# Batch 3's local q and k: transposed by DMA and reordered from SBUF, instead of transposed on TensorE

## The chip, the core and the metric

The kernel runs on one core of a Trainium2 chip. The metric is the device time of one execution in microseconds, the median of several runs. All engines of the core work from their own queues of instructions and wait for each other by semaphores: TensorE (PE, with its weight loads PEld), VectorE (DVE), ScalarE (ACT), GpSimd (POOL), which also issues the loads that cast from fp32 to bf16, and SyncE (SP), which issues DMA transposes and output stores.

## What is computed

Sparse attention over 8 batches, 8 heads, 576 tokens, 64 channels, then a feed-forward layer without bias over all 4608 tokens:

```python
scores = scale * np.matmul(q, k.transpose(0, 1, 3, 2))
rel = pos[:, None] - pos[None, :]
mask_local = (rel >= 0) & (rel < 32)                                   # heads 0 to 3
mask_strided = (rel >= 0) & (pos[None, :] % 32 == pos[:, None] % 32)   # heads 4 to 7
attn = softmax(np.where(masks, scores, -1e9))
x = np.matmul(attn, v)                  # tokens x 512
h = np.maximum(x @ w_in, 0.0)           # 512 -> 2048
out = (h * h) @ w_out                   # 2048 -> 512
```

Inputs and output are fp32; the kernel computes in bf16 with fp32 sums.

## The kernel before

A unit is a pair of heads of one batch, number 4 b + p for batch b and pair p. Pairs 0 and 1 are local (unit 12 and 13 in batch 3), pairs 2 and 3 strided. Attention writes its result, channels on partitions, into four tiles `xt`, one per pair, with 576 columns per batch. The feed-forward layer reads `xt` in nine chunks of 512 tokens.

The main loop is a list of 288 groups of four matmuls of 128x512: for each chunk 16 groups `mm1` (L707: `xt` by `w_in`; ACT's relu L713 and DVE's square L714 follow) and 16 groups `mm2` (L729: by `w_out`; after each four groups ACT copies the sum to a tile `y` at L733 and SP stores it at L737). `mm1` uses two PSUM banks in turn. Groups 32 to 47 are `mm1` of chunk 1, 48 to 63 `mm2` of chunk 1, and group 64 begins `mm1` of chunk 2.

The attention is written by hand between these groups. `PLAN` has lines "group: words", and each word runs a step just before the group's matmuls; every engine then takes its instructions in that order. A unit or batch stands behind the letter, then q or k, then the engine (a ACT, v DVE). The words that matter here:

- `l3k12+13`, `l3q12+13` (L290): POOL loads q or k of units 12 and 13 with a cast to bf16 into unused columns of `xt`, six tokens on a partition.
- `c12qa` (`cast_qk_local`, L297): ACT or DVE copies one unit's rows into a tile `q_l` or `k_l`, heads side by side.
- `T12qa` (`step_T`, L453, L460): six TensorE transposes of 96x128 into a PSUM bank, then a copy that puts the tokens in order into `qT` or `kTl`, channels on partitions.
- `S12!` (L505, L521, L527): scores of a local unit, exponentials on ACT, masks on DVE; `D12.0`, `D12.1` (L667, L672, L673) multiply by v and divide; `E12` (L682) brings the result into `xt`, for batches from 2 on by a DMA transpose on SP.
- `C3q`, `C3k` (L349): POOL loads of the strided heads' rows of a batch into one tile each for q and k, used by all batches in turn; `X3q`, `X3k` (L354): their DMA transposes on SP into `qT_s` and `kT_s`; `k30v`, `k31v` (L365, L368): DVE's copies into `kb`; `s3.0` to `s3.2` (L574): the strided scores; `x3.0` to `x3.2` (L585 to L604): the sums, their inverse and the product with v into `xt`.
- `Q16k` and the like (L278), `Y16` (L378): from batch 4 on, local q and k are loaded one token on a partition and transposed by DMA straight into place.
- `V` and `U`: loads of v; `B`: spreading them.

Tile pools hold four `q_l`, four `k_l` and four `qT`; `kTl` is four tiles, chosen by `v_slot`, `(b * 2 + p % 2) % NV`.

Of the kernel before, what the change touches and what calls it, by code (L numbers as in the profile page):

```python
# [9 lines left out]
BF16 = mybir.dt.bfloat16  # L10
# [18 lines left out]
6: o2 l2k8+9 mv0g o3 mk0g  # L29
10: c4qv  # L30
11: c4kv
12: l2q8+9 T4qa
13: c5qv c5ka T4kv
14: W1q0v T5qa
15: S4!
16: W1q1v T5ka
# [14 lines left out]
35: T8kv  # L51
37: T9kv
38: T8qv C3k
41: S8!
42: T9qa
44: S9! D8.0 k20v
45: D8.1 k21v
46: B20v
47: E8 D9.0 B21v U3
48: Q16k s2.0  # L60
49: D9.1
50: Q17q Q16q c12kv s2.1
51: c12qa E9 s2.2
52: Q17k c13kv c13qa
54: x2.0
55: X3q X3k
56: x2.1 C4k C4q
57: T12ka
58: V4 T13qv T12qa
59: T13ka  # L70
60: x2.2 B30v
61: B31v
63: U4 S12!
# [83 lines left out]
def kernel(  # L157
# [9 lines left out]
    nc = tc.nc  # L167
    B, H, S, D = q.shape
    d_model, d_ff = moe_w_in.shape
    T = B * S  # L170
# [3 lines left out]
    QL = 96  # L174
# [15 lines left out]
    qkT = ctx.enter_context(tc.tile_pool(name="qkT", bufs=4))  # L190
# [17 lines left out]
    def bank(nm):  # L208
        if places:
            return all_banks[places.pop(0)]  # L210
        t = banks[nm].pop(0)
        banks[nm].append(t)
        while id(t) in unread:
            run_due(lambda x: x[1] == unread[id(t)])
        return t
# [10 lines left out]
    NV = 4  # L226
# [12 lines left out]
    kTl = [singles.tile([128, 32 + S], BF16, name=f"kTl{i}") for i in range(NV)]  # L239
# [18 lines left out]
    units = [(b, p) for b in range(B) for p in range(H // 2)]  # L258
    st = {}
# [34 lines left out]
    def cast_qk_local(u, name, copy):  # L294
        s = st[u]
        t = qk_in.tile([QL, 6, 2, D], BF16, name=f"{name}_l")
        copy(t.rearrange("p j h d -> p h j d"), s[name + "f"].rearrange("p h (j d) -> p h j d", j=6))  # L297
        s[name] = t
# [16 lines left out]
    def step_TS(b, name, g, copy):  # L315
        src = str_rows[b, name]
        pt = bank("pt").bitcast(BF16)[:, 0:S]
        if b:
            for i in range(NJ):
                c = 128 * (NJ * g + i)  # L320
                nc.tensor.transpose(pt[:, SP_ * i:SP_ * (i + 1)], src[:, c:c + 128], ident[0:SP_, 0:SP_])
            if g == 0:
                o = strTs[name].tile([128, NP2 * SR], BF16, name=f"{name}T_s")
                str_T[b, name] = o.rearrange("c (a p) -> c a p", p=SR)
            copy(str_T[b, name][:, NJ * g:NJ * (g + 1), 0:SP_], pt.rearrange("c (a p) -> c a p", p=SP_))
            return
        for i in range(2):
            for s3 in range(NP3):
                c = 128 * (2 * g + i)
                o = S // 2 * i + QL * s3  # L330
                nc.tensor.transpose(pt[:, o:o + QL], src[:, s3, c:c + 128], ident[0:QL, 0:QL])
        if g == 0:
            o = strTs[name].tile([128, 2 * NJ * SR], BF16, name=f"{name}T_s")
            str_T[b, name] = o[:, 0:2 * NJ * SP_].rearrange("c (a r) -> c a r", a=NJ // 2)
        o = str_T[b, name]
        copy(o[:, 2 * g:2 * g + 2, :].rearrange("c a r -> c (a r)"), pt)
        if g == 1:
            for i in range(2):
                st.setdefault(2 + i, {})[name + "T"] = \
                    o[:, :, 2 * SP_ * i:2 * SP_ * (i + 1)].rearrange("c a (h p) -> c h a p", h=2)  # L340
# [11 lines left out]
    def transpose_str(b, name):  # L352
        o = strTs[name].tile([128, NP2 * SR], BF16, name=f"{name}T_s").rearrange("c (a p) -> c a p", p=SR)
        nc.sync.dma_start_transpose(out=o, in_=big.pop((b, name)))  # L354
        str_T[b, name] = o
# [14 lines left out]
    def transpose_local(u):  # L370
        s = st[u]
        for name in "qk":
            if name == "k":
                full = kTl[v_slot(u)]
                dst = full[:, 32:32 + S]
            else:
                full = dst = qkT.tile([128, S], BF16, name="qT")
            nc.sync.dma_start_transpose(out=dst.rearrange("c (t p) -> c t p", p=QL),  # L378
                                        in_=s[name].rearrange("p t h d -> p (t h d)"))
            s[name + "T"] = full  # L380

    def v_slot(u):
        b, p = units[u]
        return (b * 2 + p % 2) % NV
# [63 lines left out]
    def step_T(u, name, copy):  # L448
        s = st[u]
        src = s[name].rearrange("p j h d -> p (j h d)")  # L450
        pt = bank("pt").bitcast(BF16)[:, 0:S]
        for j in range(6):
            nc.tensor.transpose(pt[:, QL * j:QL * (j + 1)], src[:, 128 * j:128 * (j + 1)],  # L453
                                ident[0:QL, 0:QL])
        if name == "k":
            full = kTl[v_slot(u)]
            dst = full[:, 32:32 + S]
        else:
            full = dst = qkT.tile([128, S], BF16, name="qT")
        copy(dst.rearrange("c (p j) -> c p j", j=6), pt.rearrange("c (j p) -> c p j", j=6))  # L460
        s[name + "T"] = full
# [6 lines left out]
    def step_B(u, half):  # L468

        local = is_local(u)  # L470
        kn = 128 if local else SP_
        pair, both = biased[u, half] = bank_pair()
        bias = bias_l[:, half].rearrange("p t c -> p (t c)") if local else bias_s.rearrange("p t c -> p (t c)")
        for ps in pair:
            nc.tensor.matmul(ps[0:kn, 0:S // 2], ident[0:kn, 0:kn], bias,  # L475
                             start=True, stop=False, skip_group_check=True)
# [263 lines left out]
    A, V, G = nc.scalar.copy, nc.vector.tensor_copy, nc.gpsimd.tensor_copy  # L740
    ENG = {"a": A, "v": V, "g": G}
# [18 lines left out]
    def warm(n):  # L760
        if n:
            pw = bank("py")
            for _ in range(n):
                nc.tensor.matmul(pw, idle[:, 0:128], idle, start=True, stop=True)
# [7 lines left out]
    def run_step(word):  # L772
        word, _, at = word.partition("/")
        places[:] = [int(x) for x in at.split(",") if x]
        op, arg = word[0], word[1:]
        if op == "w":
            warm(int(arg))
        elif op == "c":
            cast_qk_local(int(arg[:-2]), arg[-2], ENG[arg[-1]])
        elif op == "T":  # L780
            step_T(int(arg[:-2]), arg[-2], ENG[arg[-1]])
        elif op == "W":
            step_TS(int(arg[0]), arg[1], int(arg[2]), ENG[arg[3]])
        elif op == "S":
            u, _, half = arg.rstrip("!").partition(".")
            step_S(int(u), int("!" in arg), [int(half)] if half else range(2))
        elif op == "G":
            step_G(int(arg))
        elif op == "b":
            step_B(*(int(x) for x in arg.split(".")))  # L790
        elif op == "N":
            step_N(int(arg))
        elif op == "O":
            step_O(int(arg))
        elif op in "sx":
            (step_SS if op == "s" else step_XX)(*(int(x) for x in arg.split(".")))
        elif op == "k":
            step_K(int(arg[0]), int(arg[1]), ENG[arg[2]])
        elif op == "m":
            memset_later(arg[:-1], nc.gpsimd if arg[-1] == "g" else nc.vector)  # L800
        elif op == "D":
            if "." in arg:
                u, part = arg.split(".")
                step_D(int(u), int(part))
            else:
                step_D0(int(arg))
        elif op == "E":
            step_E(int(arg.rstrip("av")), ENG.get(arg[-1]))
        elif op == "P":
            first_part(*([int(x) for x in y] for y in arg.split(".")))  # L810
        elif op == "H":
            shift_v_local(int(arg[:-1]), ENG[arg[-1]])
        elif op == "C":
            load_str_tall(int(arg[:-1]), arg[-1])
        elif op == "Q":
            load_qk_rows(int(arg[:-1]), arg[-1])
        elif op == "X":
            transpose_str(int(arg[:-1]), arg[-1])
        elif op == "Y":
            transpose_local(int(arg))  # L820
        elif op == "V":
            load_v_local_all(int(arg))
        elif op == "U":
            load_v_str(int(arg))
        elif op == "B":
            spread_v_str(int(arg[0]), int(arg[1]), ENG[arg[2]])
        elif op == "l":
            load_qk_local_sw(int(arg[0]), [int(x) for x in arg[2:].split("+")], arg[1])
        elif op == "r":
            load_str_rows(int(arg[0]), arg[1])  # L830
        elif op == "i":
            load_w_in(int(arg))
        elif op == "o":
            load_w_out(int(arg))
        elif op == "z":
            late_constants()
        else:
            raise ValueError(word)
# [143 lines left out]
```

## Time and profile before

| | |
|---|---|
| median of 3 runs | 299.3 us (299.23 to 299.55) |
| profiled execution, own time | 300.02 us |
| its span | 298.3 us |
| granted TensorE clock | 1.00 |
| PE busy | 289.5 us |
| DVE, ACT, POOL busy | 176.6, 172.2, 74.1 us |
| q0, q1: packets | 54448, 38512 |

The page gives busy times per engine over the span, the span in 40 slices of 7.46 us, the DMA queues (q0 carries POOL's loads, q1 SP's transposes and stores), the chain of waits that ended last, and the costliest groups of instructions by line. A timeline line has start, length, engine, line, operation and, in brackets, the idle time before it and what ended it. Instructions that follow each other are merged, with their number behind an x.

### The profile page before, as it was taken

The page shows a single profiled execution, that of the slowest core. Times are in us where ns is not written, and L with a number is a line of the kernel's source. Part 1 is how long each engine was busy: PE and PEld are TensorE (multiplying, and loading weights), DVE is VectorE, ACT ScalarE, POOL GpSimd, SP SyncE. Part 2 cuts the span into 40 slices and gives each one's busy share as a digit, 9 for nine tenths or more (in the row PEclk, how much of TensorE's full clock was granted, in tenths as well). Part 3 has the DMA queues.
Part 4 walks back from the last instruction along what each step waited for, and adds up shares of the span by engine and source line. Part 5 has one row for each costly group of instructions (what it writes and reads, how often), then busy time and mean ns, then how long its engine had stood idle before and what let it go on. Part 6 is the DMA issues. An engine that isn't in the chain of part 4 may idle for free.

```text
span 298.3 us, 5654 instructions
## 1 busy us (share of the span) xinstructions
PE 289.5 (97%) x2136; PEld 146.0 (49%) x2172; DVE 176.6 (59%) x457; ACT 172.2 (58%) x324; POOL 74.1 (25%) x107
## 2 busy tenths in 40 slices
PE   7989999999999999999999999999999999999996
PEld 2644555544544544444455445544454444444445
DVE  6657689668768694598267945685484534104400
ACT  3758846696667735773477547645665257126511
POOL 8973743005404008138303800000000000000000
PEclk9999999999999999999999999999999999999999
DMA  7999999999999999999997998621011110010012
GB/s 146 188 208 205 193 199 185 145 196 160 133 155 191 152 155 175 146 155 175 199 194 120 171 190 120 108 57 70 35 23 54 66 43 0 35 74 35 0 70 73
DMA packets 93131, 37.28 MB, mean 125 GB/s; under 512 B 78956, under 2 KB 87238, under 8 KB 93104
## 3 DMA queue, kind: packets, MB, share of 16 engines
q0 software_dynamic: 54448, 18.82, 59.1%
q1 hardware_dynamic: 38512, 18.03, 31.7%
q8 instruction: 17, 0.28, 0.4%
q14 instruction: 10, 0.08, 0.1%
q10 hardware_dynamic: 144, 0.07, 0.1%
HBM read 38.21 MB, written 9.44 MB: 160 GB/s over the span
## 4 chain that ended last, share of the span: by engine, by line
PE 89%; DMA 6%; issue 2%; ACT 1%; DVE 1%; SPq 0%; POOL 0%; DVEq 0%; ACTq 0%; POOLq 0%
PE psb L729 40%; PE psb L707 37%; DMA qT_s<-q_t 4%; DMA w_out_b<-in_k_dram 2%; PE psb L667 2%; PE psb L574 1%; PE psb L588 1%; PE psb L754 1%; PE psb L585 1%; PE psb L453 1%; PE psb L505 1%; PE psb L550 1%; ACT r L713 1%; DVE xt L635 0%; PE psb L475 0%
## 5 line engine op out<-in xcount | busy, mean ns | idle before, releaser
L707 PE MATMUL psb<-xt,w_in_b 128*128 128x512 bf16 x558 | 132.1, 379 | 1.2 <-DVE xt L635 0.2
L729 PE MATMUL psb<-w_out_b,g_sb 128*128 128x512 bf16 x542 | 125.3, 379 | 1.3 <-issue 0.6
L713 ACT ACTIVATE r<-psb 128x512 bf16<-128x512 f32 x144 | 85.5, 600 | 37.5 <-PE psb L707 34.0
L714 DVE TENSOR_TENSOR g_sb<-r 128x512 bf16<-128x512 bf16 x144 | 60.8, 424 | 73.6 <-ACT r L713 72.8
L707 PEld LDWEIGHTS <-w_in_b 128*128 128x128 bf16 x576 | 53.4, 98 | 58.8 <-issue 1.3
L729 PEld LDWEIGHTS <-g_sb 128*128 128x128 bf16 x560 | 51.8, 98 | 57.3 <-DVE g_sb L714 0.3
L733 ACT COPY y<-psb 128x512 f32<-128x512 f32 x35 | 20.6, 590 | 53.2 <-PE psb L729 50.2
L598 DVE TENSOR_TENSOR xt<-psb,rv 64x144 bf16<-64x144 f32 x84 | 34.1, 406 | 9.0 <-ACT rv L591 7.9
L590 ACT ACTIVATE rv<-psb 128x432 f32<-128x432 f32 (+1 forms) x21 | 10.5, 500 | 9.8 <-PE psb L585 9.8
L673 DVE TENSOR_TENSOR x_l<-psb,rinv 96x384 bf16<-96x384 f32 x28 | 15.5, 553 | 1.0
L349 POOL DMA_DIRECT2D q_t<-in_q_dram x6 | 3.2, 542 | 46.1 <-DMA qT_s<-q_t 28.2
L604 DVE TENSOR_TENSOR xt<-psb,rv 64x270 bf16<-64x270 f32 (+1 forms) x28 | 11.0, 433 | 3.7 <-ACT rv L591 3.5
L278 POOL DMA_DIRECT2D k_l<-in_k_dram x16 | 11.9, 754 | 4.2 <-ACT kTl L460 2.8
L575 ACT ACTIVATE e<-psb 128x432 bf16<-128x432 f32 (+1 forms) x21 | 10.4, 496 | 4.2 <-PE psb L574 4.0
L418 POOL DMA_DIRECT2D vl<-in_v_dram x7 | 10.1, 1442 | 6.3 <-PE psb L550 2.1
L278 POOL DMA_DIRECT2D q_l<-in_q_dram x16 | 11.6, 736 | 0.0
L561 ACT ACTIVATE e<-psb 128x384 bf16<-128x384 f32 x24 | 9.6, 509 | 3.4 <-PE psb L550 3.4
L591 ACT ACTIVATE rv<-rv 128x432 f32<-128x432 f32 (+1 forms) x21 | 11.2, 533 | 0.7
L557 DVE TENSOR_TENSOR e<-e,mask_all 128x576 bf16<-128x576 bf16 x16 | 6.7, 458 | 7.5 <-ACT e L561 7.5
L667 PEld LDWEIGHTS <-e 128*128 128x128 bf16 x168 | 8.6, 101 | 4.6
L349 POOL DMA_DIRECT2D k_t<-in_k_dram x6 | 3.4, 561 | 29.1 <-DMA kT_s<-k_t 27.2
L667 PE MATMUL psb<-vl,e 128*128 128x65 bf16 x168 | 9.5, 195 | 0.1
(117 smaller groups left out, 215.8 us busy)
## 6 DMA issues: line engine op xcount, KB each, us to landing
out_dram<-y SPq DMA_DIRECT2D x35, 256.0 KB, 3.4
vl<-in_v_dram POOLq DMA_DIRECT2D x7, 384.0 KB, 8.4
w_out_b<-in_moe_w_out_dram POOLq DMA_DIRECT2D x4, 512.0 KB, 15.5
q_t<-in_q_dram POOLq DMA_DIRECT2D x7, 288.0 KB, 5.9
k_t<-in_k_dram POOLq DMA_DIRECT2D x7, 288.0 KB, 6.5
v_st<-in_v_dram POOLq DMA_DIRECT2D x7, 216.0 KB, 8.5
w_in_b<-in_moe_w_in_dram POOLq DMA_DIRECT2D x2, 704.0 KB, 13.9
k_l<-in_k_dram POOLq DMA_DIRECT2D x16, 72.0 KB, 7.1
```

The source lines that it names most:

```text
L278: nc.gpsimd.dma_start(out=t[:, :, hh, :], in_=src[b, 2 * p + hh].rearrange("(t p) d -> p t d", p=QL))
L590: nc.scalar.activation(rv, pn, AF.Ln)
L591: nc.scalar.activation(rv, rv, AF.Exp, scale=-1.0)
L598: nc.vector.tensor_tensor(to[:, :, NJ * part:NJ * (part + 1), par], of, by, op=ALU.mult)
L604: nc.vector.tensor_tensor(t, of[:, g:, :, lo:lo + k], by[:, g:, :, lo:lo + k], op=ALU.mult)
L667: nc.tensor.matmul(po[0:m, n, :], e[:, c:c + m], rhs[:, NL * part + n, 0:D + 1], start=True, stop=True)
L673: nc.vector.tensor_tensor(x, po[0:QL, :, 0:D], rinv[0:QL].to_broadcast([QL, NL, D]), op=ALU.mult)
L707: nc.tensor.matmul(ph, w_in_b[:, kk, 128 * ff:128 * (ff + 1)], xt[kk][:, 512 * c:512 * (c + 1)], start=(kk == order[0]), stop=(kk == order ...
L713: nc.scalar.activation(r, ph, AF.Relu)
L714: later(1, lambda: nc.vector.tensor_tensor(g[:, ff, :], r, r, op=ALU.mult))
L729: nc.tensor.matmul(py, g[:, ff, 128 * j:128 * (j + 1)], w_out_b[:, ff, :], start=(ff == 0), stop=(ff == 15))
L733: nc.scalar.copy(y, py)
```

## The change

For batch 3's local units 12 and 13 the four steps T (24 TensorE transposes, four copies out of PSUM) leave groups 57 to 59. In their place `A` (`transpose_cast`) has SP transpose the cast rows by DMA into a tile in SBUF, at groups 39, 40, 42 and 43, and `R` (`order_local`) copies from that tile to the final one with the tokens in order, at groups 55 to 58. The casts move from groups 50 to 52 to groups 39, 40, 42 and 43; the two k casts now run on ACT and the two q casts on DVE, where before DVE cast k and ACT cast q. The transposed k goes into the `kTl` tile two further on, the transposed q into an own tile of the `qT` pool; from batch 3 on the `kTl` slots are shifted by two (`k_slot`). The cast of unit 5's q moves from group 13 to group 12. TensorE's order has 24 matmuls and 24 weight loads fewer and is otherwise the same; SP's has four DMA transposes more, behind `X2q` and one store and ahead of `E8`; POOL's loads keep their order.

```diff
-12: l2q8+9 T4qa
-13: c5qv c5ka T4kv
+12: l2q8+9 T4qa c5qv
+13: c5ka T4kv
...
+39: c12ka A12k
+40: c13ka A13k
 41: S8!
-42: T9qa
+42: T9qa c12qv A12q
+43: c13qv A13q
...
-50: Q17q Q16q c12kv s2.1
-51: c12qa E9 s2.2
-52: Q17k c13kv c13qa
+50: Q17q Q16q s2.1
+51: E9 s2.2
+52: Q17k
 54: x2.0
-55: X3q X3k
-56: x2.1 C4k C4q
-57: T12ka
-58: V4 T13qv T12qa
-59: T13ka
+55: X3q X3k R12kv
+56: x2.1 C4k C4q R12qa
+57: R13ka
+58: V4 R13qv
...
-                full = kTl[v_slot(u)]
+                full = kTl[k_slot(u)]
...
+    def transpose_cast(u, name):
+
+        t = kTl[(k_slot(u) + 2) % NV][:, 32:32 + S] if name == "k" else qkT.tile([128, S], BF16, name="qT")
+        nc.sync.dma_start_transpose(out=t.rearrange("c (j p) -> c j p", p=QL),
+                                    in_=st[u][name].rearrange("p j h d -> p (j h d)"))
+        st[u][name + "6"] = t
+
+    def order_local(u, name, copy):
+        s = st[u]
+        if name == "k":
+            full = kTl[k_slot(u)]
+            dst = full[:, 32:32 + S]
+        else:
+            full = dst = qkT.tile([128, S], BF16, name="qT")
+        copy(dst.rearrange("c (p j) -> c p j", j=6), s[name + "6"].rearrange("c (j p) -> c p j", j=6))
+        s[name + "T"] = full
+
+    def k_slot(u):
+
+        return (v_slot(u) + 2 * (units[u][0] > 2)) % NV
...
+        elif op == "A":
+            transpose_cast(int(arg[:-1]), arg[-1])
+        elif op == "R":
+            order_local(int(arg[:-2]), arg[-2], ENG[arg[-1]])
```

More of the change, by code (lines that the diff above doesn't have):

```diff
@@ L455, in step_T @@
         if name == "k":
-            full = kTl[v_slot(u)]
+            full = kTl[k_slot(u)]
             dst = full[:, 32:32 + S]
```

## The prediction

> **What bounds the kernel now.** I read the page first: busy times, then the slices.
>
> ```profile
> PE 289.5 (97%) x2136; PEld 146.0 (49%) x2172; DVE 176.6 (59%) x457; ACT 172.2 (58%) x324; POOL 74.1 (25%) x107
> DMA  7999999999999999999997998621011110010012
> ```
>
> TensorE is busy for 97% of the span, so the order written for it is nearly the time: what is taken off PE is gained, unless something then lands late. The second line says where that can happen: up to about 186 us (25 slices of 7.46 us) the DMA engines are full. The change removes PE work near 80 us and adds DMA work near 65 us, inside that stretch. So next I read the chain of waits there, in order of time (start, length, what).
>
> ```profile
> 57.00 11.70 DMA qT_s<-q_t
> 68.74 0.36 PE psb L574 x8
> ...
> 78.20 0.26 PE psb L453 x6
> ...
> 79.32 0.51 PE psb L453 x12
> ...
> 80.70 0.26 PE psb L453 x6
> ```
>
> The three L453 pieces are the 24 transposes of T12k, T12q, T13q, T13k: 0.26 + 0.51 + 0.26 = 1.03 us, all on the chain. The first line is a DMA transpose, X2q, already just too late: PE's own waits give 0.36 us for it at step s2.0. Then SP's timeline, which shows the queue that the new transfers enter:
>
> ```profile
> 57.00 5.09 SPq L354 DMA_TRANSPOSE qT_s<-q_t  x1
> 62.14 0.58 SPq L737 DMA_DIRECT2D out_dram<-y  x1
> 67.53 6.01 SPq L682 DMA_TRANSPOSE xt<-x_l  x2
> 73.74 0.41 SPq L737 DMA_DIRECT2D out_dram<-y  x1
> 74.26 3.65 SPq L354 DMA_TRANSPOSE qT_s<-q_t  x1
> 78.00 4.88 SPq L354 DMA_TRANSPOSE kT_s<-k_t  x1
> ```
>
> These are X2q, an output, E8 and E9, an output, X3q, X3k. In the DMA view's issues, read in narrow windows, E8 lands 3.5 us after its issue (71.0), E9 8.4 (80.7), X3q 11.9 (86.2), X3k 11.5 (89.5): in the order of issue, and slowly from 72 us on. Last, the timelines of DVE and PE show who uses X3k:
>
> ```profile
> 89.51 0.38 DVE L365 COPY kb<-kT_s 64x864 bf16<-64x864 bf16 x1 [0.37 <-DMA kT_s<-k_t]
> 91.38 0.24 DVE L368 COPY kb<-kT_s 64x324 bf16<-64x324 bf16 x1
> 92.94 0.36 PE L574 MATMUL psb<-qT_s,kb 128*128 128x54 bf16 x8
> ```
>
> DVE starts step k30 in the moment X3k lands; k31 ends at 91.62; PE reaches s3.0 at 92.94. X3k has 1.3 us of slack, and no more.
>
> **The change, part by part.**
>
> *Transposes off PE.* 24 matmuls with their weight loads leave, 1.03 us. On both sides of them PE runs main matmuls without gaps, so nothing covered them: -1.03.
>
> *Two k casts onto ACT at groups 39 and 40.* Their data lands at 57.3 (issue 42.24 plus 15.1), before they stand at the head of ACT's queue, about 59.3. A cast of this form takes 0.82 us on ACT; the instruction behind it starts 0.73 later (51.58, then 52.31). Queued behind them are two of ACT's relu steps, L713, and the four exponentials of S8; main matmuls of group n+2 wait for the relu of group n, since two banks are used in turn. Before, the relu of group 39 starts at 59.64, of 40 at 60.51, the exponentials at 61.00, the relu of 41 at 62.16. With the casts, by the same starts (0.49 for a relu, 0.73 for a cast): cast 59.27, relu 60.00, cast 60.49, relu 61.22, exponentials 61.71, relu of 41 at 62.87. ACT's gaps of 0.27 before relu 39 and before relu 40 take most of the rest of the 1.46. So group 43, which starts as that relu ends (62.80 before), starts 0.7 later: PE loses 0.7. It reaches s2.0 at 69.1 instead of 68.38, when X2q (68.74) has landed, so the old wait of 0.36 goes. Net +0.34. Ends: 0 (the gaps hide more) and 1.65 (both casts in full).
>
> *Two q casts onto DVE at groups 42 and 43.* Data lands at 61.5 (46.98 plus 14.5); they stand at about 63.5 and 64.6. 0.35 each, 0.70; DVE has gaps of 0.64, 0.24 and 0.25 there, and the masks of S8 behind them lead PE's D8.0 and D8.1 by over 1.5 us. Nothing. If the data were a microsecond later, DVE would wait, and those masks still be in time.
>
> *Casts and PSUM copies leave groups 50 to 59; four SBUF copies come.* ACT loses two casts (1.65) and three copies of 0.64 and gets two copies; DVE loses two casts (0.70) and a copy of 0.75 and gets two. No row has a copy from SBUF that gathers with a step of 96 elements. Nearest rows: for 576 elements, ACT 0.62 (scaled from L297, 0.82 for 768) to 0.64 (L460); DVE 0.26 (L297 scaled) to 0.75 (L460). A gather could be slower than either; doubled, 1.3 to 1.5, it is still covered: ACT idles over 2.5 us between 79 and 85, and what the copies feed, S12, starts at 84.64, when the last copy of before has been over for 2.6 us (DVE, 82.04). I take the rows, and nothing on the path.
>
> *Batch 1's q cast one group sooner.* Weight loads of L453 waited for DVE's q casts twice, 0.3 in all, 0.2 at most; part of that is this cast. Between -0.2 and +0.1 (a square step L714 0.35 later): I take -0.1.
>
> *Four DMA transposes onto SP.* They stand between the output at 62.14 and E8. SP is idle from 62.72 to 67.53, each issue costs it 1.2 us when nothing is in its way (E8), 3 to 5 under load (X2k, X2q, X3q). Every later SP entry moves behind them: E8, E9, the output, X3q, X3k. POOL's loads C4k and C4q wait for X3k and X3q, and so move with them. X2q stands ahead and isn't touched.
>
> The price is packets. One such transpose is 608 packets (an E step, of the same size, alone in the DMA view at 219.7 us); four are 2,432. Room: from 69 to 71 the hardware queue q1 moved 495 packets; from 102 to 104, with the software queue q0 nearly silent, it moved 1,805, so 1,310 more could go. From 71 to 73 q1 was empty, while q0 brought rows of 4 KB; in 73 to 80, with the same loads, q1 made 637 packets, 91 a microsecond, so some 180 more. That leaves 940. From 80 on the two queues share evenly:
>
> ```profile
> q0 software_dynamic: 1184, 0.15, 80.4%
> q1 hardware_dynamic: 1159, 0.30, 79.3%
> ```
>
> (85.2 to 88 us: packets, MB, share.) q1 gets 414 packets a microsecond, so 940 are 2.3 us: X3k lands at 91.8. k30 and k31 end 2.1 us after it, as before, at 93.9. PE, by then 0.8 us earlier than before (-1.03 + 0.34 - 0.1), would be there at 92.15. The wait is 1.7 us, since the slack of 1.3 is down to 0.5 when PE comes earlier. Ends: nothing (room for all) and 2,432 / 414 = 5.9 less 0.5, 5.4. I take 1.7 since both rooms are read from the same microseconds.
>
> [...] In 102 to 104 us transposes ran at 0.45 MB in 2 us, 225 GB/s, alone; beside the row loads at 85.2 to 88, 0.30 MB in 2.8 us, 107 GB/s. [...]
>
> [...] All twelve xt<-x_l transposes, of the shape added here, land in a median of 3.1 us, the fastest in 2.5. [...]
>
> *Sum.* -1.03 + 0.34 - 0.1 + 1.7 = +0.9. The profiled execution took 300.02 us (span 298.3, 1.7 around it) and becomes 300.9; it stands 0.7 above the median of 299.3, to which the same difference applies: 300.2.
>
> **The rivals.**
>
> *Hidden.* The backlog drains before X3k: what SP had already queued could start while X2q's last packets run, before 69, and q1 may do more than 91 packets a microsecond in 71 to 80, where only one transfer stood in it. It decides at X3k's landing: up to 90.0 PE waits for nothing, and the sum is -0.8: 298.5. For: the gaps of DMA near 70, 74 and 77 us. Against: E9, alone in its queue, took 8.4 us there. Chance 0.28.
>
> *Half of it.* X3k lands between 90.2 and 91.4, or ACT pays both casts in full (+1.65) while X3k is in time: between -0.6 and +0.6, near 299.5. Chance 0.17.
>
> *No room at all.* If the four stand in front of E8 and E9 while the row loads run, everything moves by up to 5.9. E9's result is first needed by group 64 at 85.9, and it landed at 80.7; past 4.5 us late PE waits there already, and R13qv holds DVE ahead of L604, which the same group needs. The two waits don't add, the last one counts: -0.8 + 5.4 gives 303.9; half way, 302. Chance 0.10.
>
> *Slow transposes.* If each of the four takes what E9 took, 8.4 us, one after the other, the last lands at 62.7 + 33.6 = 96.3, and S12, due at 84, waits some 12: about 310. The median landing of 3.1 speaks against it. Chance 0.02. [...]
>
> The forecast itself, X3k late by 2 to 3 us, 299.9 to 301.1, gets 0.43.
>
> **How the numbers follow.** Told from no change, within 0.2%, is 298.7 to 299.9. Slower: 0.43 + 0.10 + 0.02 = 0.55; same 0.17; faster 0.28. Most likely is 300.2, with a range of its own from 299.9 to 301.1. The range of 8 in 10 goes down into the hidden case, to 298.3, and up to 302.4, half way into the case without room.
>
> **What would show it.** L453's 24 pieces gone from 78 to 81 us; group 43 later by 0.7 and no wait for X2q at s2.0; E9 landing 2 us later than 80.7; DVE waiting about 3 us before L365 for X3k, and PE a wait of 1.7 at s3.0. X3k at 90 or sooner would prove me wrong, as would a wait of ACT or DVE for one of the four new transposes.

## The result and the profile after

The changed kernel takes 301.29 us (median of six runs, 300.62 to 302.22); the kernel before, run beside it, 299.67 (six runs, 299.23 to 300.11). The ratio is 1.0056, with a 95% interval of 1.0035 to 1.0077: slower by 1.6 us, where 0.9 was forecast. (Ratios here leave disturbed runs out, so one need not equal the quotient of the two medians.) The profiled execution took 302.22, with a span of 300.5.

The page of the changed kernel has nearly the same two lines as before, PE at 97% and DMA full for the first 25 slices. (PE's count is higher than before, though 24 matmuls are gone, because the trace of before lacks records: its page has 558 and 542 matmuls of `mm1` and `mm2`, this one has all 576 and 560.)

```profile
PE 291.3 (97%) x2148; PEld 145.0 (48%) x2148; DVE 177.8 (59%) x458; ACT 172.4 (57%) x323; POOL 74.7 (25%) x107
DMA  7999999999999999999998999511011100010012
```

The chain of waits in order of time shows other links, however. (All line numbers of the changed kernel are higher: L299 is the cast, L730 and L752 are `mm1` and `mm2`, L597 the strided scores, L573 the local ones from batch 4 on.)

```profile
58.86 0.39 ACT k_l L299
...
60.18 0.33 ACT k_l L299
...
63.12 1.02 PE psb L730 x4
...
78.72 12.21 DMA kT_s<-k_t
...
90.95 0.38 DVE kb L367
...
92.96 0.38 PE psb L597 x8
```

The three L453 pieces are gone. In their place the two casts of k on ACT stand on the chain, and then one DMA transpose, X3k, with 12.2 us of it. SP's timeline shows the four new transposes (L387) and what follows them:

```profile
56.33 4.22 SPq L356 DMA_TRANSPOSE qT_s<-q_t  x1
60.60 0.58 SPq L760 DMA_DIRECT2D out_dram<-y  x1
61.30 4.18 SPq L387 DMA_TRANSPOSE kTl<-k_l  x2
65.57 3.12 SPq L387 DMA_TRANSPOSE qT<-q_l  x2
68.79 5.01 SPq L705 DMA_TRANSPOSE xt<-x_l  x2
...
75.38 3.24 SPq L356 DMA_TRANSPOSE qT_s<-q_t  x1
78.72 5.49 SPq L356 DMA_TRANSPOSE kT_s<-k_t  x1
```

They land at 70.7, 71.3, 71.9 and 75.1. Behind them E8 lands at 79.3 (71.0 before), E9 at 81.5 (80.7), X3q at 87.2 (86.2), X3k at 90.9 (89.5). At s3.0 DVE, and PE behind it, now wait for X3k (timelines of DVE and PE; idle time and its releaser in brackets):

```profile
90.95 0.38 DVE L367 COPY kb<-kT_s 64x864 bf16<-64x864 bf16 x1 [3.06 <-DMA kT_s<-k_t]
92.96 0.38 PE L597 MATMUL psb<-qT_s,kb 128*128 128x54 bf16 x8 [1.03 <-DVE kb L367]
```

PE's waits over the span (in total, times, longest) name one more place:

```profile
PE psb L597 <- DVE kb L367: 1.0, 1, 1.0
PE psb L573 <- DMA kTl<-k_l: 0.9, 1, 0.9
PE psb L730 <- ACT r L736: 0.6, 1, 0.6
```

The last is group 43 behind ACT's casts. The middle one is at group 121 (G5), the local scores of unit 21, 50 us behind the change; no step of the prediction has it. (Some of the expectations call it batch 2's; unit 21 is of batch 5.)

To see where time comes and goes I compare the starts of ACT's copies of `y` (L733 before, L756 after) one by one, in ACT's timelines. Two of them, before:

```profile
81.86 0.59 ACT L733 COPY y<-psb 128x512 f32<-128x512 f32 x1 [0.23 <-PE psb L729]
...
106.09 0.59 ACT L733 COPY y<-psb 128x512 f32<-128x512 f32 x1 [0.81 <-PE psb L729]
```

and in the changed kernel, which is 1.29 ahead at the first, with TensorE relieved, and 0.03 behind at the second, with s3.0 between them:

```profile
80.57 0.59 ACT L756 COPY y<-psb 128x512 f32<-128x512 f32 x1
...
106.12 0.59 ACT L756 COPY y<-psb 128x512 f32<-128x512 f32 x1 [0.81 <-PE psb L752]
```

Each column below is the start in that kernel's trace less the start in the trace of before; the head names the time before.

| kernel | 49.6 | 73.1 | 81.9 | 106.1 | 140.9 | 145.0 | last |
|---|---|---|---|---|---|---|---|
| changed kernel | -0.41 | -0.26 | -1.29 | +0.03 | +0.03 | +1.15 | +1.16 |
| again | +0.18 | +0.33 | -0.70 | +0.75 | +1.47 | +1.78 | +1.78 |
| casts_only | +0.33 | +0.49 | +0.49 | +0.49 | +0.49 | +0.49 | +0.49 |
| casts_and_dma | +0.51 | +0.67 | +0.67 | +0.67 | +0.66 | +0.67 | +0.67 |
| k_casts_dve | -0.09 | -0.61 | -1.64 | +0.29 | +0.29 | +1.58 | +1.58 |
| x3k_first | -0.19 | -0.04 | -1.08 | -0.03 | +1.93 | +2.08 | +2.08 |
| half | +0.11 | +0.26 | -0.25 | -0.25 | -0.25 | +1.48 | +1.47 |
| y21_early | -0.30 | -0.15 | -1.17 | +0.86 | +0.85 | +0.86 | +0.85 |
| before_again | +0.90 | +0.38 | +0.38 | +0.39 | +0.39 | +0.96 | +0.96 |
| before_y21_late | +0.46 | -0.06 | -0.06 | -0.06 | -0.06 | +2.69 | +2.69 |
| before_y21_early | +1.20 | +0.68 | +0.69 | +0.69 | +0.69 | +0.69 | +0.69 |
| half_plain | +0.98 | +0.45 | -0.06 | -0.06 | -0.06 | -0.06 | -0.06 |

The first row is the result's account: from 49.6 to 73.1 us the ACT casts less the vanished wait for X2q, +0.15; T gone, -1.03; s3.0, +1.32; G5, +1.12. The first column varies between executions of one and the same kernel (0 and +0.90 for before). The other 1.0 of the span's difference of 2.2 lies behind the last copy. About 0.8 of it is the last store, which lands 2.35 us after its issue, 1.56 in the trace of before. The repeat below has 2.36, but five other versions with all four DMA transposes issued have 1.6, so I don't count this against the change. Why both executions of the changed kernel have it isn't known.

### The profile page after: what moved, and what is told of

Read it like the earlier page. It is cut to its first block, busy times and chain, and to the rows that moved or that the text cites. A ratio compares the mean times of both kernels' runs of the same rounds, so it can differ in the third digit from the quotient of the medians.

```text
span 300.5 us, 5652 instructions
## 1 busy us (share of the span) xinstructions
PE 291.3 (97%) x2148; PEld 145.0 (48%) x2148; DVE 177.8 (59%) x458; ACT 172.4 (57%) x323; POOL 74.7 (25%) x107
## 3 DMA queue, kind: packets, MB, share of 16 engines
q1 hardware_dynamic: 40944, 18.62, 32.8%
## 4 chain that ended last, share of the span: by engine, by line
PE 85%; DMA 7%; DVE 3%; ACT 2%; SPq 1%; issue 1%; DVEq 0%
PE psb L730 37%; PE psb L752 35%; DMA kT_s<-k_t 4%; DMA kTl<-k_l 3%; PE psb L690 2%; PE psb L787 1%; PE psb L597 1%; PE psb L611 1%; PE psb L777 1%; PE psb L528 1%; PE psb L476 1%; PE psb L608 1%; ACT r L736 1%; PE psb L573 1%; PE psb L498 1%
## 5 line engine op out<-in xcount | busy, mean ns | idle before, releaser
L730 PE MATMUL psb<-xt,w_in_b 128*128 128x512 bf16 x576 | 133.6, 379 | 1.0 <-ACT r L736 0.6
L752 PE MATMUL psb<-w_out_b,g_sb 128*128 128x512 bf16 x560 | 127.6, 379 | 0.0
L730 PEld LDWEIGHTS <-w_in_b 128*128 128x128 bf16 x576 | 53.4, 98 | 59.4 <-issue 2.0
L752 PEld LDWEIGHTS <-g_sb 128*128 128x128 bf16 x560 | 52.0, 98 | 58.0 <-DVE g_sb L737 0.3
L756 ACT COPY y<-psb 128x512 f32<-128x512 f32 x35 | 20.6, 590 | 53.4 <-PE psb L752 53.2
L627 DVE TENSOR_TENSOR xt<-psb,rv 64x270 bf16<-64x270 f32 (+1 forms) x28 | 10.9, 430 | 2.5 <-ACT rv L614 2.2
L597 PEld LDWEIGHTS <-kb 128*128 128x128 bf16 x154 | 6.8, 96 | 6.0 <-DVE kb L367 1.5
```

The costliest lines, as they stand in the source:

```text
L627: nc.vector.tensor_tensor(t, of[:, g:, :, lo:lo + k], by[:, g:, :, lo:lo + k], op=ALU.mult)
L730: nc.tensor.matmul(ph, w_in_b[:, kk, 128 * ff:128 * (ff + 1)], xt[kk][:, 512 * c:512 * (c + 1)], start=(kk == order[0]), stop=(kk == order ...
L752: nc.tensor.matmul(py, g[:, ff, 128 * j:128 * (j + 1)], w_out_b[:, ff, :], start=(ff == 0), stop=(ff == 15))
L756: nc.scalar.copy(y, py)
```

## The experiments

The versions were timed in four groups, each beside runs of before of its own. Between groups only the ratios compare, not the medians.

**again.** The changed kernel once more, no edit.

> The changed kernel once more, for a second profile and an interval. First profile: a wait of PE of 0.61 us for ACT at group 43, of 1.03 at s3.0 behind X3k (landed 90.9), and of 0.94 at G5 (L573) behind the transposed k of Y21, which the forecast did not have. Backlog theory: the first two come again, within 0.3 us each. Knock-on theory: the wait at G5 comes again too, 0.5 to 1.5 us; if it was chance, G5 waits for nothing and the span is about 1 us shorter. Time against before: 1.003 to 1.008.

Measured: 301.26 (299.83 to 307.58, twelve runs) beside 299.88 for before; ratio 1.0033 (0.9992 to 1.0073), so this interval, unlike the first, reaches no change. The repeat shows the same wait for X3k (1.1; it landed at 91.6), and waits for the k of later units again: 0.7 for unit 16's at 112.9, 0.3 for unit 21's. The size and place of these waits move from one execution to the next.

**casts_only.** The casts where the change has them, the transposes by TensorE in their old place.

```diff
-39: c12ka A12k
-40: c13ka A13k
+39: c12ka
+40: c13ka
...
-42: T9qa c12qv A12q
-43: c13qv A13q
+42: T9qa c12qv
+43: c13qv
...
-55: X3q X3k R12kv
...
+55: X3q X3k
```

(T12 and T13 stand at groups 57 to 59 again.)

> The four casts stand early as in the changed kernel, but TensorE transposes as before (no DMA transposes, no SBUF copies). Backlog theory: the wait for ACT at group 43 of about 0.6 is there, X2q's wait at s2.0 is gone, nothing waits at s3.0: +0.1 to +0.4 us against before (ratio 1.000 to 1.0015). ACT theory (the early casts are what costs): +1 us or more (1.003 and up).

Measured: 300.31 (300.00 to 302.23), ratio 1.0003 (0.9982 to 1.0025). Its trace has the 0.6 for ACT's relu and no new wait behind it; X3k lands at 89.6. So the early casts alone cost 0.8 us at most, by the interval, and leave X3k where it was.

**casts_and_dma.** As before, but the four `A` stay in as well; their tiles aren't read.

```diff
-55: X3q X3k R12kv
-56: x2.1 C4k C4q R12qa
-57: R13ka
-58: V4 R13qv
+55: X3q X3k
+56: x2.1 C4k C4q
+57: T12ka
+58: V4 T13qv T12qa
+59: T13ka
```

> As casts_only, and SP also issues the four DMA transposes at groups 39 to 43; nobody reads their result, TensorE still transposes. The price of the transfers alone. Backlog theory: X3k lands 1.5 to 2.5 us later than in casts_only, PE comes to s3.0 1 us later than in the changed kernel, so waits 0 to 0.7 there: 0 to +0.7 against casts_only, and a wait at G5 may be added (0 to 1). ACT theory: same as casts_only.

Measured: 301.30 (300.45 to 306.81), ratio 1.0040 (1.0015 to 1.0064), 1.0 above casts_only by the medians. In its trace E8 is late as in the changed kernel (79.1) but X3k lands at 89.8, only 0.2 after casts_only's. PE, which still has the T steps, reaches s3.0 only at 93.6, and so would have borne an X3k up to 91.6. The 1.0 is thus not in this trace, and what the other executions lost was not seen. It stays open, and with it whether the four transfers cost time in a way that isn't the wait at s3.0.

**c3k_first.** The strided k of batch 3 loaded and transposed ahead of the q.

```diff
-34: C3q
+34: C3k
...
-38: T8qv C3k
+38: T8qv C3q
...
-55: X3q X3k R12kv
+55: X3k X3q R12kv
```

> The changed kernel with batch 3's strided k loaded and transposed ahead of its q (C3k and C3q change places, X3k and X3q too). Backlog theory: X3k lands by 88 instead of 90.9, DVE's k30 and k31 are in time, the wait of 1.03 at s3.0 goes, X3q lands near 91 and is just in time: 0.7 to 1.0 us faster than the changed kernel, if nothing later takes it back. Knock-on theory: Y21's landing near 143 stays, PE comes to G5 a microsecond earlier and waits nearly 2 there, so less than 0.3 us is gained.

Measured: 309.25 (304.82 to 312.18), ratio 1.0256 (1.0194 to 1.0318). It went far off. C3k may go out as soon as X2k has landed, at 63.4, while C3q in that place waited for X2q until 68.4. So a load of 288 KB enters the queues 5 us sooner, just where the four transposes are: they land at 75.9 to 87.8, E8 at 90.4, E9 at 92.0, and group 64 waits for both. PE's waits:

```profile
PE psb L730 <- DMA xt<-x_l: 5.1, 2, 4.1
PE psb L528 <- ACT qT L398: 1.4, 1, 1.4
```

This is the prediction's rival "no room at all" with the place that it named (E9, group 64), brought about by a load instead of by the transposes alone. The waits are not all of the 9 us: the granted clock was 0.5 from 86.9 to 97.1 us (0.983 as the mean over the span), where eight matmuls of `mm1` took 3.60 us (from 93.60 on); sixteen took 3.79 in the changed kernel (from 88.14 on), at a granted clock of 1.0.

**k_casts_dve.** The two k casts on DVE.

```diff
-39: c12ka A12k
-40: c13ka A13k
+39: c12kv A12k
+40: c13kv A13k
```

> The changed kernel with the two k casts at groups 39 and 40 on VectorE in place of ScalarE. Theory 1 (the 0.6 that PE waits for ScalarE's relu at group 43 is the casts' price, of which 0.36 comes back because the wait for the strided q transpose of batch 2 is gone): that wait goes, the later wait for batch 2's q transpose comes back at up to 0.36, and the time falls by 0.2 to 0.4 against the changed kernel, to about 301.0. Rival (VectorE has no room at groups 39 and 40 either): a wait of 0.3 to 0.6 for VectorE in place of ScalarE's, time unchanged or 0.3 longer. Rival (only the late DMA loads count): the wait goes and the end does not move by more than 0.1, because the chunk that follows waits for its loads anyway.

Measured: 301.21 (299.40 to 308.83) beside 300.16; ratio 1.0020 (0.9989 to 1.0050); against 1.0056 and 1.0033 for the changed kernel, no gain that stands clear of the spread. The wait for ACT is gone, and from 49.6 to 73.1 it does as the kernels with the old casts do, -0.52 instead of +0.15. At s3.0 that came to nothing:

```profile
PE psb L597 <- DVE kb L367: 1.6, 1, 1.6
PE psb L573 <- DMA kTl<-k_l: 1.1, 1, 1.1
```

X3k landed at 91.2, and PE started s3.0 2.0 us after it, as in the changed kernel (92.96 after 90.93). While X3k binds, whatever PE saves ahead of it is only a longer wait. This is the third reading on record, that only the late loads count.

**x3k_first.** Only the two strided transposes exchanged on SP.

```diff
-55: X3q X3k R12kv
+55: X3k X3q R12kv
```

> The changed kernel with one pair of SP's instructions exchanged: batch 3's strided k transpose goes ahead of its strided q transpose. Theory 1 (PE's wait at the first scores of batch 3, 1.0 in the profile of the changed kernel, comes from the k transpose landing at 90.9 as the last of SP's row): k now lands at 87 to 89, q takes its place at 90 to 91.5, the wait of PE for VectorE's ordering copy falls to between 0 and 0.3 unless q, which is needed at about the same group, takes it over; the time falls by 0.5 to 1.0 against the changed kernel, to about 300.5. Rival (the row as a whole is late and either order meets it): a wait of the same 0.8 to 1.1 for the q transpose in its place, time unchanged at 301.3. Rival (knock-on waits in later batches set the end): the wait goes but the later waits for the local k of batch 2 take it back, time unchanged, with 1 to 1.5 of wait at these.

Measured: 300.87 (299.80 to 312.94) beside 300.16, ratio 1.0033 (0.9999 to 1.0066). X3k lands at 89.5, X3q at 92.9. PE's waits:

```profile
PE psb L573 <- DMA kTl<-k_l: 1.9, 1, 1.9
...
PE psb L597 <- DMA qT_s<-q_t: 0.7, 1, 0.7
```

Of s3.0's wait 0.7 is left, now for q, and the later one is longer (unit 16's k, landed at 113.4). It is the row that is late, not one transfer in it, and an exchange inside it mends little.

**half.** Only unit 12 by DMA; unit 13's early casts stay, its transposes are TensorE's.

```diff
-40: c13ka A13k
+40: c13ka
...
-43: c13qv A13q
+43: c13qv
...
-57: R13ka
-58: V4 R13qv
+58: V4 T13qv
+59: T13ka
```

> The changed kernel with only one unit's q and k (unit 12's) by DMA; unit 13's cast rows are transposed by TensorE again, in two steps at groups 58 and 59. Theory 1 (a backlog in SP's row by the packet: four transposes cost 2.3 to 1.4 of lateness at the last strided k transpose): with two the k transpose of batch 3 lands at 89.6 to 90.3 and PE's wait at the first scores of batch 3 is 0 to 0.5; TensorE keeps 0.5 of the 1.0 that it was relieved of; time about 300.4, between the kernel before and the changed one. Rival (the price is not in the transposes but in the early casts on ScalarE, 0.6 of wait at group 43): time about 301.0, close to the changed kernel. Rival (no backlog at all below some number of transposes): wait zero and the later waits in batch 2's band scores gone, time 299.8, no longer than before.

Measured: 300.86 (299.80 to 306.33) beside 300.16, ratio 1.0024 (0.9990 to 1.0057). SP's timeline has a gap again between A12q and E8, X3k lands at 89.7, and s3.0 has no wait; TensorE's relief is 0.51. All of this as the backlog theory has it. But its trace has a longer wait at G5 than the changed kernel's, though its row up to 95 us is on time:

```profile
143.35 0.43 PE L573 MATMUL psb<-qT,kTl 64*128 64x96 bf16 x12 [1.55 <-DMA kTl<-k_l]
```

So the wait at G5 is no consequence of a late row at s3.0, and needed an experiment of its own.

**y21_early.** The local transposes of unit 21 (Y21) two groups sooner, ahead of E16 on SP.

```diff
-102: Q25q V5 E16
+102: Q25q V5 Y21 E16
...
-104: Y21 s4.1
+104: s4.1
```

> The changed kernel with the local transposes of unit 21 issued at group 102, ahead of batch 5's unit 16 loads in SP's row, in place of group 104. Theory 1 (the 0.9 that PE waited at the band scores for the local k of batch 2 is the late landing, 142.98 where before it was 138.67): it lands some 3 to 5 sooner, that wait goes, and the time falls by 0.4 to 0.9 against the changed kernel, to about 300.7. Rival (the wait is passed on: the row loads that now come behind it are late instead): the wait goes at that place and 0.5 to 1 of wait comes back for the loads of unit 16 or the unit behind it, time unchanged at 301.3. Rival (the wait differs between executions and is mostly hidden): time within 0.2 of the changed kernel's.

Measured: 301.27 (299.71 to 304.20) beside 300.16, ratio 1.0044 (1.0013 to 1.0074). Unit 21's k lands at 140.6 in place of 143.0 and the wait is gone, with nothing in its place up to the end (the row of the table is flat behind 106.1). The time did not fall; X3k landed at 91.7 in this trace and took 2.0. That the earlier place takes the wait away is shown, a gain in time is not.

**before_again, before_y21_late.** Is the wait at G5 the change's at all? The kernel before once more, and the kernel before with Y21 one step later on SP:

```diff
-104: Y21 s4.1
+104: s4.1
...
-111: E17
+111: E17 Y21
```

> The kernel before, unchanged, a second time beside itself. Theory 1 (the waits at the first scores of batch 3 and at the band scores of unit 21 belong to the change): neither is in its trace (0.4 at most), and its time is within 0.3 of the runs of the kernel before. Rival (such waits come and go between executions of any version): one of them, of 0.7 or more, is in this trace too.

> The kernel before, without any part of the change, but with the local transposes of unit 21 one step later in SP's row (behind unit 17's row load), so that GpSimd's load of V for batch 5 goes out ahead of them, as it did in the changed kernel. Theory 1 (what makes unit 21's k late is its place in the queue behind that load): k lands at 142 to 145, PE waits 0.5 to 2 at unit 21's band scores, and the time is 0.4 to 1.5 above that of the kernel before. Rival (it is late because the loads of the whole stage come later after the change): k lands some 1.3 later than in the kernel before, at 140, which the slack of 3 swallows; no wait, time the same within 0.3.

Measured: before_again 299.81 (299.20 to 304.08), ratio 0.9992 (0.9969 to 1.0015); its trace has 0.4 at G5, the most that the first theory allows, so such a wait can come without the change. before_y21_late: 302.95 (299.36 to 305.12) beside 299.97, ratio 1.0051 (1.0015 to 1.0086). The timelines of POOL, SP and PE of the latter:

```profile
131.62 1.44 POOL L418 DMA_DIRECT2D vl<-in_v_dram  x1
133.90 1.29 SPq L378 DMA_TRANSPOSE kTl<-k_l  x1
144.56 0.43 PE L550 MATMUL psb<-qT,kTl 64*128 64x96 bf16 x12 [2.57 <-DMA kTl<-k_l]
```

A wait of 2.6 us, more than expected, without any part of the change: POOL's load of V for batch 5 (384 KB) goes out 2.3 us ahead of the transpose, which lands 10.6 us after its issue instead of 5.7 (and is also issued 0.9 us later than in the trace of before). By the timelines and the DMA issues of the traces:

| kernel | V load issued | unit 21's k issued | landed | after | PE waits |
|---|---|---|---|---|---|
| before | 133.9 | 133.0 | 138.7 | 5.7 | 0 |
| half_plain | 130.4 | 129.2 | 134.9 | 5.7 | 0 |
| before_y21_early | 131.7 | 131.0 | 137.0 | 6.0 | 0 |
| y21_early | 133.6 | 132.5 | 140.6 | 8.0 | 0 |
| again | 135.3 | 135.7 | 143.6 | 7.9 | 0.3 |
| casts_only | 131.2 | 132.1 | 140.5 | 8.3 | 0 |
| casts_and_dma | 130.8 | 132.1 | 141.6 | 9.4 | 0 |
| x3k_first | 134.6 | 134.8 | 143.9 | 9.1 | 0.1 |
| before_again | 131.0 | 131.9 | 142.8 | 10.9 | 0.4 |
| changed kernel | 132.7 | 133.4 | 143.0 | 9.6 | 0.9 |
| k_casts_dve | 132.6 | 133.5 | 143.4 | 9.9 | 1.1 |
| half | 130.4 | 132.3 | 143.3 | 11.0 | 1.5 |
| before_y21_late | 131.6 | 133.9 | 144.5 | 10.6 | 2.6 |
| c3k_first (9 us late as a whole) | 141.2 | 141.6 | 149.4 | 7.8 | 0 |

Ahead of the V load it takes 5.7 to 8.0, behind it 7.8 to 11.0; PE waits only in traces where it is behind, though not in all of them. Which goes first hangs on POOL: its V load follows a load that waits for X5k to have read `k_t`. X5k landed at 131.4 in the trace of before and at 129.9 in the changed kernel's, and POOL was free 1.5 us sooner:

```profile
130.45 0.82 POOL L351 DMA_DIRECT2D k_t<-in_k_dram  x1 [8.37 <-DMA kT_s<-k_t]
...
132.74 1.44 POOL L441 DMA_DIRECT2D vl<-in_v_dram  x1
```

(Changed kernel, POOL's timeline.) It isn't X5k's landing alone: in the repeat X5k landed at 132.7, later than in before, and the V load still went first, since SP came to unit 21's k only at 135.7. So a shift of 1.6 us between the two queues lets a large load overtake a small transpose that PE needs first (V's load is issued 0.9 us behind unit 21's k in the trace of before, 0.7 ahead of it in the changed kernel's). The same order came up in a trace of the unchanged kernel; whether the change makes it more frequent can't be told from one trace per kernel.

**half_plain.** Put together from this: unit 12 alone by DMA, its k cast on DVE, unit 13 as in before, Y21 at group 102. Against before (`k_slot`, the new steps and the sooner cast of unit 5's q included):

```diff
+39: c12kv A12k
...
-42: T9qa
+42: T9qa c12qv A12q
...
-50: Q17q Q16q c12kv s2.1
-51: c12qa E9 s2.2
+50: Q17q Q16q s2.1
+51: E9 s2.2
...
-55: X3q X3k
-56: x2.1 C4k C4q
-57: T12ka
-58: V4 T13qv T12qa
+55: X3q X3k R12kv
+56: x2.1 C4k C4q R12qa
+58: V4 T13qv
...
-102: Q25q V5 E16
+102: Q25q V5 Y21 E16
-104: Y21 s4.1
+104: s4.1
```

> A version put together from what the runs showed: only unit 12's q and k by DMA, its k cast on VectorE at group 39, unit 13 wholly as in the kernel before, and the local transposes of unit 21 at group 102. Theory 1 (the prices of the change are the ScalarE casts, the backlog of four transposes and the place of unit 21's transposes; half of TensorE's relief is 0.5): no wait for ScalarE's relu at group 43, none at the first scores of batch 3, none at unit 21's band scores; time 0.2 to 0.6 below the kernel before, about 299.5. Rival (the executions' spread and the load on the DMA queues eat a gain of this size): within 0.3 of the kernel before. Rival (two transposes already cost what they bring, in a wait at another place): 0.3 to 1 above it.

Measured: 299.49 (299.13 to 301.70) beside 299.97; ratio 0.9982 (0.9960 to 1.0004). It has none of the three waits, its X3k lands at 89.5, and between 73.1 and 81.9 us it gains 0.51, which it keeps to the end. It is the only changed version with a ratio below 1, 0.5 below before by the medians; the interval just reaches no change, so a gain is likely and not established.

**before_y21_early.** How much of that is Y21's place: before with that edit alone (the diff of y21_early).

> The kernel before with one edit: the local transposes of unit 21 at group 102 in place of 104, and nothing of the change. It tells which part of the last version's 0.5 is TensorE's relief. Theory 1 (the relief of 0.5 by unit 12's DMA transposes is real, and the earlier place of unit 21's transposes takes away only a wait that some executions have): no wait at unit 21's band scores, time between 299.6 and 299.9, 0 to 0.3 below the kernel before. Rival (the place of unit 21's transposes is all of it): time 299.4 to 299.5, as in the last version. Rival (unit 17's row load, now behind them, comes late): a wait of 0.3 or more for it, time 300 or above.

Measured: 300.44 (299.52 to 304.02) beside 299.64; ratio 1.0016 (1.0005 to 1.0027). No wait at G5, and none for unit 17's row, as the first theory says; but the time lies 0.8 above before, which neither it nor the others forecast. In its trace all of the difference (+0.69) stands ahead of 73 us, where this edit does nothing, so its cause isn't known. It gives no sign that the lower time of half_plain is Y21's place.

## Why the prediction was right, and where it wasn't

It came out slower, as forecast, by 1.6 where 0.9 was forecast, and the traces show the mechanism forecast: a DMA row at s3.0 that takes back what TensorE gains. The forecast steps do not make up all of the 1.6, and that their sum fits is partly luck. The result, 301.29, lies 0.2 above the range given for the forecast itself and inside the wide one. Step by step:

*Transposes off PE, -1.03.* Exact: -1.03 in the changed kernel, -0.51 in both versions with half of it.

*Two k casts on ACT, +0.34.* The wait at group 43 is there (0.6, forecast 0.7), and the one for X2q is gone. The step is mis-sized all the same: from 49.6 to 73.1 us every trace with the casts on ACT has +0.15 or +0.16, and every one with the casts of k on DVE or in their old place but before's own has -0.52 or -0.53. The price is 0.67, the 0.7 of the step's working. The 0.36 given back for X2q belongs to that one execution of before, where X2q landed at 68.7 (67.9 in k_casts_dve's); no other trace of those kernels has that wait.

*Unit 5's q cast, -0.1.* The right sign. The first column averages +0.64 over the four traces with the old order (0, 0.90, 0.46, 1.20), +0.12 over the nine of the table with the new one; single executions spread by more than 1, so the size stays open.

*SBUF copies, nothing.* Right on the path, though ACT needs 1.16 us for one (forecast 0.64, at most 1.5) and DVE 0.65; nobody waits for them in the changed kernel's trace.

*Four transposes, X3k 2.3 late, a wait of 1.7.* The packets are as counted: q1 has 40,944, 2,432 more. The waits are 1.0, 1.1, 1.6 and 1.6 in the four traces that keep SP's order and have the T steps gone, with X3k at 90.9 to 91.7, 1.4 to 2.3 late; two transposes (1,216 packets) leave it at 89.5 to 89.7, with no wait at s3.0. The forecast is at the upper end. X3k's landing alone does not prove the room counted, though: casts_and_dma has it at 89.8 with all four, and before_again and before_y21_early have it at 90.3 and 91.1 with none. The path is also another one than the prediction's. It had SP's entries pushed back behind the four, but SP had caught up by E9 (issued at 72.6, 72.3 before). What came late was POOL's load C3q, which took 6.9 us instead of 4.4 while the four were under way (casts_only and casts_and_dma, which differ in the four alone, have 5.3 and 7.6). X3q can't be issued before this load lands, and SP waited for it in every trace with four transposes and this order of q and k, in no other. (Landings and issues from the DMA issues of the traces, the wait from SP's own waits.)

| kernel | new transposes | C3q landed | SP's wait | X3q issued | X3k landed |
|---|---|---|---|---|---|
| before | 0 | 73.7 | 0 | 74.3 | 89.5 |
| before_y21_late | 0 | 73.6 | 0 | 74.7 | 89.5 |
| before_again | 0 | 72.7 | 0 | 75.2 | 90.3 |
| before_y21_early | 0 | 73.2 | 0 | 75.5 | 91.1 |
| casts_only | 0 | 74.2 | 0 | 75.3 | 89.6 |
| half | 2 | 74.0 | 0 | 75.0 | 89.7 |
| half_plain | 2 | 74.5 | 0 | 75.2 | 89.5 |
| casts_and_dma | 4 | 75.6 | 0.3 | 75.7 | 89.8 |
| changed kernel | 4 | 75.3 | 0.9 | 75.4 | 90.9 |
| k_casts_dve | 4 | 76.9 | 2.8 | 77.0 | 91.2 |
| again | 4 | 77.2 | 2.1 | 77.2 | 91.6 |
| y21_early | 4 | 77.0 | 2.5 | 77.1 | 91.7 |

Where PE goes on is then X3k's landing and 2.0 us, so TensorE's 1.03 and ACT's 0.67 are both settled there: +0.03, +0.75, +0.29 and +0.86 at 106.1 us.

*The sum.* From 49.6 to 106.1 us the changed kernel's terms are 0.67 - 1.03 + 1.32 = 0.96 against the three traces of before_again, before_y21_late and before_y21_early, and 0.44 against the trace of before shown above, which has the wait for X2q. The casts cost 0.33 more than forecast and s3.0 0.38 less, and the two errors cancel: that is luck.

*What was missed* is the rest: 0.9 at G5 (1.12 in the table of copies), unit 16's and 21's k in the repeat. The prediction followed SP's row to X3k and stopped, taking what lay behind as unmoved. These waits may be what carries the median from +0.9 to +1.6, but that is not shown: the wait at G5 comes and goes in the unchanged kernel too (0 and 0.4), the late last store adds 0.8 to both traces of the changed kernel, y21_early took the wait at G5 away without a lower time, and casts_and_dma lost its 1.0 without a wait at s3.0 in its trace.

*The landing of the four.* Four transposes of 0.6 MB were issued from 61.3 and landed by 75.1, 6.4 to 9.4 us each from issue to landing, with other transfers on the DMA engines; the median of the transposes of E in the trace of before is 3.1. The rival of slow transposes, with the last of them at 96.3, is not what the trace shows.

*What would show it* was met in the main, with a wait of 1.0 instead of 1.7 at s3.0, but E9 came 0.8 later instead of 2: it was E8, 8.3 later, that took the delay, and its reader comes at 85.9.

## What to carry to other kernels

Ahead of a full DMA row, a microsecond taken off the busiest engine was worth nothing here once a transfer bound (1.03 us off TensorE, and +0.03 at 106.1 us). Count the packets added against the room left before the first transfer with little slack, and move only as many as fit (here two transposes of four, by the traces: X3k at 89.5 to 89.7 with two, at 90.9 to 91.7 with four where SP's order was kept and the T steps were gone). Look at the other queue's loads too: here the added transposes delayed a load (C3q, 6.9 us instead of 4.4), and SP, with the transfer of little slack next in its order, waited for that load (0.9 us). Then go on along the queues: in the changed kernel X5k landed 1.5 us sooner, V's load of 384 KB went out ahead of unit 21's k instead of behind it, and that transpose took 9.6 us instead of 5.7, far from the edit. Check a small loss or gain against a second trace of the unchanged kernel, for part of the waits in one trace belong to that execution (at G5, 0 in one trace of the unchanged kernel and 0.4 in the other).

## What the runs showed of the hardware

A DMA transpose of one unit's k (608 packets) took 5.7 to 8.0 us from issue to landing when issued up to 1.3 us ahead of a 384 KB row load on POOL's queue, 7.8 to 11.0 when issued up to 2.3 us behind it, though the two are in different queues. A 288 KB load on POOL's queue (C3q, issued at 67.9 to 68.8 us) took 6.9 to 8.5 us beside four such transposes, and 4.4 to 5.5, issued at 68.4 to 69.3, beside none or two. A copy within SBUF that gathers tokens with a step of 96 took ACT 1.16 us, against 0.64 for the copy out of PSUM that it replaced; on DVE it took 0.65 against 0.76.
